# Scores and float32 folds as 64-row by 32-column products, and the first batch's k and v as two tensors

## The chip, the cores and the metric

The program runs on one core of a Trainium2 chip. The metric is the device time of one execution in microseconds (us); the kernel before takes 704.06 us, the median of three runs from 703.98 to 704.45. The core has a matrix engine (TensorE, PE in the profile; its weight loads are listed apart as PEld), two engines for elementwise work (VectorE is DVE, ScalarE is ACT), GpSimd (POOL) and SyncE (SP), whose queue issues most of the loads from memory. Each engine runs its own list of instructions in the order in which they stand there, and waits on semaphores for the others.

## The reference

Eight batches with eight heads of 576 tokens (head size 64) attend to 32 memory slots per head; the output goes through a feed-forward layer with g = h·cos(h).

```python
a = softmax(phi, axis=2)                       # phi: b, h, s, m (m = 32)
k_m = einsum('bhsm,bhsd->bhmd', a, k)          # memory keys
v_m = einsum('bhsm,bhsd->bhmd', a, v)          # memory values
scores = matmul(q, k_m.transpose(0, 1, 3, 2)) / sqrt(64)
attn_out = matmul(softmax(scores), v_m)        # b, h, s, d
x = attn_out as (b*s, 512)
h = x @ w_in                                   # 512 x 2048
out = (h * cos(h)) @ w_out                     # 2048 x 512
```

The two weights come as float64. phi, q, k and v are float32, and q, k and phi are scaled up so that both softmaxes are sharp.

## The kernel before, in words

The matrix of memory values is never applied to the attention weights. It is folded into `w_in` instead: for every batch the products v_m · w_in give a matrix of 256 rows (8 heads of 32 slots) by 2048 columns (`vw`, for the first group `vf`), and the softmaxed scores, transposed (`aT`), are multiplied by it directly. That is the first large product (`gemm1`, tile `hp`, L529 and L538). ACT and DVE then build h·cos(h) (`act`, `act_end`, tiles `u` and `gp`), and `gemm2` (tile `acc`, L577 and L582) multiplies by `w_out`. Group 0 does this in float32; the eleven later groups use pairs of float16 numbers, three products for one.

The 4608 tokens form 12 groups of 384. For each group the main loop takes 16 steps, one for each 128 of the 2048 hidden columns. A step issues `gemm1`, the two activations of `act`, and `gemm2` for the step four before it (`LAG`). Between the steps of group 0 the weights are converted from float64 to float32 (`to_float32`: a cast L147, an or L152, a square for the scale L155) in an order given by the list `todo`. Each converted piece of 256 columns of `w_in` is folded at once (`fold_first`, L500, tile `pvf`, copied to `vf` at L502). Batch 1 folds in float32 from the converted `w_in` (`fold` and `fold_psum`, L470); batches 2 to 7 fold with float16 pairs (L476).

The preparation of a batch is two generators, `memory` and `attend`, whose `yield`s cut them into 24 parts. Jobs with a first and a last step spread these parts over the steps of the groups before. `memory` makes the softmax of phi and the products with k and v (tile `psA`: 32 output rows per head, in four column quarters of the matrix array), divides by the sum (`den`, `X`), transposes (`tpx`), and writes the memory keys `km` and values `vm`. Both are laid out block-diagonally for pairs of heads: 128 rows by 64 columns per pair, where half of the entries are zeros that POOL sets beforehand (L300, L301). `attend` makes the scores (L381, tile `sc`): one product per pair of heads with all 128 rows of `km`, 64 output rows each, so that two products lie side by side in the array. It takes three blocks of tokens of 256, 256 and 64 (first batch: 256, 128 and 192), and the four products of one block lie in one bank of the pool `ps_s`. DVE transposes them back in 32 by 32 squares (L386), and the softmax over the 32 slots follows (L394 to L405).

The pool `ps_s` has two banks. `psA`, `tpx`, `sc`, `pvf` and `pv` all take their banks from it, and a new tile waits until the tile two before it has been read.

Before the loop stands the start-up, written out by hand: loads in the order phi, kv, q (first 384 tokens), `w_in` 0, `w_in` 1, the rest of q, `w_out` 0; then the first batch's `memory`, the conversion of `w_in` 0, the scores of its first 384 tokens, their softmax, `fold_first(0)` and `fold_first(1)`. Between them stand products of zeros (`warm`, L633) that keep the matrix engine busy. A scheduler then sets the final order on every engine by its own estimates; a few instructions are pinned.

## Time and profile before

The profiled execution took 702.34 us; the span of its core, from the first to the last instruction, is 700.6 us, so 1.7 us lie around it.

| what | value |
|---|---|
| median of the runs | 704.06 us |
| profiled execution | 702.34 us |
| span of the core | 700.6 us |
| PE busy | 685.8 us (98%) |
| DVE busy | 527.0 us (75%) |
| ACT busy | 500.0 us (71%) |
| POOL busy | 25.1 us (4%) |
| first product of the main loop (`hp`, group 0) starts | 31.03 us |
| granted clock over the span | 0.995 |

A busy share is the time in which at least one instruction of that engine ran. A float32 product appears as two records on PE, and products in different parts of the array overlap. The view by windows gives the busy time of each engine in stretches of the span; the chain of waits is followed back from the last instruction and gives start, length and what ran.

### The profile page before, as it was taken

The numbers are of one execution on the slowest core, as the hardware profiler recorded it, in microseconds if no ns is written. First come the engines' busy times: TensorE is split into PE (matmuls) and PEld (weight loads), VectorE is DVE, ScalarE is ACT, GpSimd is POOL, SyncE is SP. The second block draws the span as 40 slices with busy tenths as digits, with TensorE's granted clock in tenths as the row PEclk, the third lists the DMA queues.
The fourth block names the chain that finished last, engine by engine and source line by source line (L and its number), as shares of the span: only waits on it lengthen the run. The fifth ranks groups of instructions, "written<-read, shape, count | busy, mean of one in ns | idle before, by whom it ended". The sixth has DMA issues, their size and how long they took to land.

```text
span 700.6 us, 11828 instructions
## 1 busy us (share of the span) xinstructions
PE 685.8 (98%) x4597; PEld 364.0 (52%) x4597; DVE 527.0 (75%) x1125; ACT 500.0 (71%) x932; POOL 25.1 (4%) x42
## 2 busy tenths in 40 slices
PE   8799999999999999999999999999999999999997
PEld 3354445665454445665445455666445445665553
DVE  4788998998969866698658876599667976665652
ACT  1598998987876765877665965778666975765652
POOL 5020000000000000000001000000000000000000
PEclk9899999999999999999999999999999999999999
DMA  8996883336224100440105300160100100100101
GB/s 270 391 330 215 291 298 88 87 93 206 80 87 153 46 0 1 148 138 1 46 1 171 113 0 1 65 220 1 46 0 2 45 1 1 46 1 1 46 1 45
DMA packets 27863, 66.18 MB, mean 94 GB/s; under 512 B 2208, under 2 KB 12320, under 8 KB 25760
## 3 DMA queue, kind: packets, MB, share of 16 engines
q1 hardware_dynamic: 23344, 57.43, 24.7%
q10 hardware_dynamic: 4464, 8.00, 3.1%
q8 instruction: 36, 0.59, 0.3%
q14 instruction: 19, 0.16, 0.1%
HBM read 51.79 MB, written 9.44 MB: 87 GB/s over the span
## 4 chain that ended last, share of the span: by engine, by line
PE 68%; DVE 14%; ACT 13%; DMA 2%; issue 1%; SPq 0%; ACTq 0%; POOL 0%
PE acc L582 34%; PE hp L538 18%; PE acc L577 5%; ACT u L557 3%; PE hp L529 3%; DVE u L561 3%; DVE u L552 3%; PE psA L275 2%; DVE gp L564 2%; PE pv L476 2%; ACT gp L563 2%; PE sc L381 2%; DMA kv<-in_kv 1%; DVE vw L483 1%; ACT gp L549 1%
## 5 line engine op out<-in xcount | busy, mean ns | idle before, releaser
L582 PE MATMUL acc<-wo,gp 128*128 128x512 f16 x1584 | 371.4, 379 | 0.4 <-ACT ob L606 0.4
L582 PEld LDWEIGHTS <-gp 128*128 128x128 f16 x1584 | 153.4, 98 | 161.6 <-issue 2.8
L538 PE MATMUL hp<-aT,vw 128*128 128x192 f16 (+1 forms) x1440 | 202.8, 284 | 1.0 <-DVE u L561 0.9
L538 PEld LDWEIGHTS <-vw 128*128 128x128 f16 x1440 | 128.3, 98 | 77.8 <-issue 18.0
L557 ACT ACTIVATE u<-u,quarter 128x384 f32<-128x384 f32 x192 | 116.5, 613 | 65.7 <-DVE u L552 64.7
L561 DVE SCALAR_TENSOR_TENSOR u<-hp,u 128x384 f32<-128x384 f32 x176 | 96.6, 554 | 60.9 <-ACT u L557 60.3
L552 DVE SCALAR_TENSOR_TENSOR u<-hp,cu,gp 128x192 f32<-128x192 f32 (+1 forms) x240 | 118.9, 504 | 23.6 <-ACT gp L549 23.1
L549 ACT ACTIVATE gp<-hp,cu 128x192 int32<-128x192 f32 (+1 forms) x240 | 115.0, 490 | 27.3 <-PE hp L538 13.0
L564 DVE TENSOR_TENSOR gp<-u,gp 128x384 f16<-128x384 f32 x176 | 96.4, 553 | 42.9 <-ACT gp L563 41.9
L563 ACT CAST gp<-u 128x384 f16<-128x384 f32 x176 | 88.6, 509 | 54.0 <-DVE u L561 52.9
L577 PE MATMUL acc<-wo,gp 128*128 128x512 f32 x96 | 44.5, 598 | 0.0
L483 DVE SCALAR_TENSOR_TENSOR vw<-pv,vw 128x512 f16<-128x512 f32 x48 | 31.5, 685 | 3.0 <-ACT vw L482 2.9
L529 PE MATMUL hp<-aT,vf 128*128 128x384 f32 x64 | 25.3, 526 | 2.5 <-DVE aT L411 2.2
L482 ACT ACTIVATE vw<-pv 128x512 f16<-128x512 f32 x48 | 26.8, 588 | 1.1 <-PE pv L476 0.9
L577 PEld LDWEIGHTS acc<-wo,gp 128*128 128x128 f32 x96 | 17.5, 190 | 18.2 <-issue 16.0
L606 ACT ACTIVATE ob<-acc,os 128x512 f32<-128x512 f32 x27 | 17.8, 681 | 9.7 <-PE acc L582 7.1
L275 PE MATMUL psA<-kv,phi 128*32 128x129 f32 (+1 forms) x640 | 21.0, 275 | 1.2 <-DMA kv<-in_kv 0.5
L557 ACT ACT_TABLE_LOAD x17 | 21.8, 1283 | 0.3
L381 PE MATMUL sc<-q,km 128*64 128x256 f32 (+3 forms) x192 | 19.1, 334 | 1.2 <-DVE vw L483 0.7
L275 PEld LDWEIGHTS psA<-kv,phi 128*32 128x32 f32 (+1 forms) x640 | 16.4, 109 | 7.3 <-issue 2.1
L529 PEld LDWEIGHTS hp<-aT,vf 128*128 128x128 f32 x64 | 12.4, 203 | 14.2 <-issue 5.6
L381 PEld LDWEIGHTS sc<-q,km 128*64 128x64 f32 x192 | 11.7, 136 | 11.1 <-issue 3.2
(136 smaller groups left out, 524.6 us busy)
## 6 DMA issues: line engine op xcount, KB each, us to landing
kv<-in_kv SPq DMA_DIRECT2D x32, 516.0 KB, 6.9
raw_out<-in_w_out SPq DMA_DIRECT2D x8, 1024.0 KB, 5.8
q<-in_qT SPq DMA_DIRECT2D x7, 1152.0 KB, 5.5
out<-ob ACTq DMA_DIRECT2D x30, 256.0 KB, 2.1
raw_in<-in_w_in SPq DMA_DIRECT2D x6, 1024.0 KB, 10.3
phi<-in_phi SPq DMA_DIRECT2D x8, 512.0 KB, 5.9
w_in_sb<-w_in_parts SPq DMA_DIRECT2D x12, 256.0 KB, 4.1
kv<-in_kv SPq DMA_DIRECT2D x8, 258.0 KB, 7.8
```

What stands on the lines that cost most here:

```text
L275: nc.tensor.matmul(psA[32 * j:32 * (j + 1), g * KV:(g + 1) * KV], lhsT=a[:n, c, h * M:(h + 1) * M], rhs=kvs[c][:n, h * KV:(h + 1) * KV], s ...
L381: nc.tensor.matmul(sc[D * p:D * (p + 1), g * n:(g + 1) * n], lhsT=km[:, 2 * g + p], rhs=qt[:, 2 * g + p, t0:t0 + n], start=True, stop=True)
L529: nc.tensor.matmul(hp[:, :GT], lhsT=st["vf", q][:, g, fo * P:(fo + 1) * P], rhs=st["aTf"][:, g], start=(g == 0), stop=(g == 1))
L538: nc.tensor.matmul(hp[:, c0:c0 + n], lhsT=vw[:, wi, g, fo * P:(fo + 1) * P], rhs=aT[:, ai, g, c1:c1 + n], start=(k == 0), stop=(k == 5))
L549: ins = nc.scalar.activation(ni[:, c], hp[:, c], AF.Copy, scale=cu, bias=0.25)
L552: nc.vector.scalar_tensor_tensor(out=u[:, c], in0=hp[:, c], scalar=cu, in1=ni[:, c], op0=ALU.mult, op1=ALU.subtract)
L557: nc.scalar.activation(u, u, AF.Sin, scale=TWO_PI_BELOW, bias=quarter)
L561: nc.vector.scalar_tensor_tensor(out=u, in0=hp[:, :GT], scalar=2.0 ** -17, in1=u, op0=ALU.mult, op1=ALU.mult)
L563: nc.scalar.copy(gp[:, 0], u)
L564: nc.vector.tensor_tensor(out=gp[:, 1], in0=u, in1=gp[:, 0], op=ALU.subtract)
L577: nc.tensor.matmul(accs[grp][t], lhsT=gp[:, t * P:(t + 1) * P], rhs=wo[:, f + 1], start=(f == 0), stop=(f == NF - 1))
L582: nc.tensor.matmul(accs[grp][t], lhsT=gp[:, gi, t * P:(t + 1) * P], rhs=parts[:, wi], start=(f == 0 and gi == 0 and wi == 0), stop=(f == N ...
```

## The change

- **Products in eighths of the array.** `km` and `vm` lose their zeros: each head has 64 rows and 32 columns, even heads in one row half, odd heads in the other. A score product takes one head: 64 rows, 32 output rows. The two row halves write to different banks, so a block of scores takes both banks of `ps_s`. The blocks are two of 288 tokens (first batch: 384 and 192). The float32 folds (`fold_single`, for `fold_first` and for batch 1) are made in the same way, also with both banks; `fold_first` copies one bank on ACT and one on DVE. The number of these products doubles, each has half the rows and half the output rows. The float16 folds only take their heads in another order. The memsets of `km` and `vm` on POOL fall away.
- **k and v of the first batch.** Two new inputs hold k with its column of ones (65 columns per head) and v (64 per head). k is loaded before q and `w_in` 0, v behind `w_in` 0. `memory_first` makes the products with k alone, then `km`; the products with v follow behind the scores, in banks of the pool `ps_acc`, and `vm` is made on ACT. `den`, `X` and the scale of the values follow from the two parts.
- **Start-up.** The order by hand is written anew and has 43 products of zeros for 51; the conversion of `w_in` 0 is no longer pinned to the middle of `memory`.

The diff, cut to its core:

```diff
-BLK = [(0, 256), (256, 256), (512, 64)]
-BLK_FIRST = [(0, 256), (256, GT - 256), (GT, S - GT)]
+BLK = [(0, 288), (288, 288)]
+BLK_FIRST = [(0, GT), (GT, S - GT)]
...
+    def load_first(src, c0, c1):
+        if c0 == 0:
+            loads["kv", 0] = [ld.tile([P, H * KV], F32, tag="kv", name=f"kv_0_{c}", bufs=5) for c in range(5)]
+        for c, (s0, n) in enumerate(TCH):
+            nc.sync.dma_start(out=loads["kv", 0][c][:n, c0:c1], in_=src[s0:s0 + n])
...
+    def memory_first():
...
+        def products(ps, c, c0, w):
+            s0, n = TCH[c]
+            for g in range(2):
+                for j in range(4):
+                    h = 4 * g + j
+                    nc.tensor.matmul(ps[32 * j:32 * (j + 1), g * w:(g + 1) * w], lhsT=a[:n, c, h * M:(h + 1) * M],
+                                     rhs=kvs[c][:n, c0 + h * w:c0 + (h + 1) * w],
+                                     start=(c == 0 and g == 0), stop=(c == 4), skip_group_check=True)
+
+        psk = small_ps("psk")
+        for c in range(5):
+            products(psk, c, 0, K1)
+            yield
...
+        km = wk.tile([P, NP, M], F32, tag="km", name=f"km_{b}", bufs=1)
+        nc.scalar.mul(km[lo], tv[lo, :, 0], 1.0 / math.sqrt(D))
+        nc.vector.tensor_scalar(out=km[hi], in0=tv[hi, :, 1], scalar1=1.0 / math.sqrt(D), scalar2=None, op0=ALU.mult)
+        st["km", 0] = km
+        yield
+        psv = ps_acc.tile([P, DM], F32, tag="ps_acc", name="psv")
+        for c in range(5):
+            products(psv, c, H * K1, D)
+            if c == 2:
+                yield
+        X = wk.tile([P, 2, P], F32, tag="back", name="X_v", bufs=4)
+        for g in range(2):
+            nc.scalar.activation(X[:, g].rearrange("p (t d) -> p t d", t=2),
+                                 psv[:, g * D:(g + 1) * D].unsqueeze(1).broadcast_to([P, 2, D]), AF.Copy,
+                                 scale=den[:, g:g + 1])
...
     def memory(b):
...
-        km = wk.tile([P, NP, 2 * M], F32, tag="km", name=f"km_{b}", bufs=1)
-        vm = wk.tile([P, NP, 2 * M], F32, tag="vm", name=f"vm_{b}")
-        nc.gpsimd.memset(km, 0.0)
-        nc.gpsimd.memset(vm, 0.0)
+        km = wk.tile([P, NP, M], F32, tag="km", name=f"km_{b}", bufs=1)
+        vm = wk.tile([P, NP, M], F32, tag="vm", name=f"vm_{b}")
...
         def score_products(i):
             t0, n = BL[i]
-            sc_at[i] = sc = small_ps(f"sc_{b}_{t0}")
-            for g in range(2):
-                for p in range(2):
-                    nc.tensor.matmul(sc[D * p:D * (p + 1), g * n:(g + 1) * n], lhsT=km[:, 2 * g + p],
-                                     rhs=qt[:, 2 * g + p, t0:t0 + n], start=True, stop=True)
+            sc_at[i] = sc = [small_ps(f"sc_{b}_{t0}_{g}") for g in range(2)]
+            for c in range(NP):
+                for g in range(2):
+                    rows = slice(g * D, (g + 1) * D)
+                    nc.tensor.matmul(sc[g][M * c:M * (c + 1), :n], lhsT=km[rows, c],
+                                     rhs=qt[rows, c, t0:t0 + n], start=True, stop=True)
...
+    def fold_single(b, name, c0, n):
+        pv = [small_ps(f"{name}_{g}") for g in range(2)]
+        for c in range(NP):
+            for g in range(2):
+                rows = slice((1 - g) * D, (2 - g) * D)
+                nc.tensor.matmul(pv[g][M * c:M * (c + 1), :n], lhsT=st["vm", b][rows, c],
+                                 rhs=w_in_sb[rows, c, c0:c0 + n], start=True, stop=True)
         return pv
...
-        (nc.scalar.copy if j < 2 else nc.vector.tensor_copy)(out=st["vf", q][:, :, r * WS:(r + 1) * WS], in_=pv)
+        pv = fold_single(0, f"pvf_{j}", j * WS, WS)
+        nc.scalar.copy(out=st["vf", q][:, 0, r * WS:(r + 1) * WS], in_=pv[0][:, 0:WS])
+        nc.vector.tensor_copy(out=st["vf", q][:, 1, r * WS:(r + 1) * WS], in_=pv[1][:, 0:WS])
...
     load_phi(0)
-    load_kv(0)
+    load_first(k_first, 0, H * K1)
     load_q(0)
     load_w_in(0)
+    load_first(v_first, H * K1, H * KV)
     load_w_in(1)
...
-    convert_w_in(0, attention_rest)
-    for _ in mem:
-        pass
+    next(mem)
+    convert_w_in(0)
     first = attend(0)
     next(first)
-    warm(12)
+    warm(4)
+    next(mem)
+    warm(2)
+    next(mem)
+    next(mem)
+    warm(2)
     fold_first(0)
     warm(6)
     next(first)
+    for _ in mem:
+        pass
```

How the scheduler's order moves is shown at three places. The first is DVE around the first scores. `sc` are the scores, `at` their transposed copy, `raw_in` the raw `w_in` 0, `X_k` and `km` the scaled and transposed memory keys. Before, then with the change:

```order
L170 TENSOR_SCALAR ev_244<-ev_244 128x1
L386 STREAM_TRANSPOSE at_248<-sc_0_251 128x512
L147 CAST w_in_sb<-raw_in_117 128x4x256
L386 STREAM_TRANSPOSE at_248<-sc_256_257 128x256
L152 SCALAR_TENSOR_TENSOR w_in_sb<-raw_in_117,w_in_sb 128x4x256
L394 TENSOR_REDUCE rm_249<-at_248 128x24
L395 TENSOR_TENSOR at_248<-at_248,rm_249 128x768
```

```order
L284 TENSOR_SCALAR X_k<-psk,den_215 128x128 x2
L154 CAST w_in_sb<-raw_in_117 128x4x256
L295 TENSOR_SCALAR km_227<-tpx_k 64x128
L159 SCALAR_TENSOR_TENSOR w_in_sb<-raw_in_117,w_in_sb 128x4x256
L470 STREAM_TRANSPOSE at_234<-sc_0_0_237 128x384
L470 STREAM_TRANSPOSE at_234<-sc_0_1_238 128x384
L478 TENSOR_REDUCE rm_235<-at_234 128x24
L479 TENSOR_TENSOR at_234<-at_234,rm_235 128x768
```

The cast of `w_in` 0 now stands ahead of one half of `km`, so ahead of the scores, and the or behind it ahead of both transposes.

The second place is DVE in the second half of the same softmax (`rs` are its sums, `aT` the transposed weights for which the first `hp` waits). Before, then with the change:

```order
L399 TENSOR_REDUCE rs_250<-at_248 128x24
L152 SCALAR_TENSOR_TENSOR w_in_sb<-raw_in_119,w_in_sb 128x4x256
L400 TENSOR_SCALAR rs_250<-rs_250 128x24
L147 CAST wo<-raw_out_122 128x1024
L401 RECIPROCAL rs_250<-rs_250 128x24
L152 SCALAR_TENSOR_TENSOR wo<-raw_out_122,wo 128x1024
L405 TENSOR_TENSOR at_248<-at_248,rs_250 128x768
L411 STREAM_TRANSPOSE aT_247<-at_248 128x256 x2
```

```order
L485 RECIPROCAL rs_236<-rs_236 128x24
L579 COPY vf_317<-pvf_1_319 128x256
L489 TENSOR_TENSOR at_234<-at_234,rs_236 128x768
L159 SCALAR_TENSOR_TENSOR w_in_sb<-raw_in_124,w_in_sb 128x4x256
L495 STREAM_TRANSPOSE aT_233<-at_234 128x384 x2
L154 CAST wo<-raw_out_127 128x1024
L579 COPY vf_317<-pvf_1_349 128x256
L159 SCALAR_TENSOR_TENSOR wo<-raw_out_127,wo 128x1024
```

The conversion of `w_out` 0 (`raw_out`) has moved from ahead of `aT` to behind it; the or of `w_in` 1 still stands ahead of it.

The third place is PE at the start of group 0. Before, then with the change:

```order
L529 MATMUL hp_0_336<-aT_247,vf_275 128x384 x2
L529 MATMUL hp_1_375<-aT_247,vf_275 128x384
L500 MATMUL pvf_352<-w_in_sb,vm_226 64x256 x4
L381 MATMUL sc_384_358<-q_115,km_225 64x192 x4
L529 MATMUL hp_1_375<-aT_247,vf_275 128x384
L529 MATMUL hp_2_405<-aT_247,vf_275 128x384 x2
```

```order
L654 MATMUL acc_1_595<-wo,gp_0_392 128x512
L464 MATMUL sc_384_0_416<-q_115,km_227 32x192 x4
L654 MATMUL acc_2_596<-wo,gp_0_392 128x512
L464 MATMUL sc_384_1_417<-q_115,km_227 32x192 x4
L338 MATMUL top_450<-ident,nmx_448 128x128 x2
L606 MATMUL hp_4_585<-aT_233,vf_403 128x384
L556 MATMUL pvf_0_463<-w_in_sb,vm_302 32x256 x4
L606 MATMUL hp_4_585<-aT_233,vf_403 128x384
L556 MATMUL pvf_1_464<-w_in_sb,vm_302 32x256 x4
```

The score block of 192 tokens and one of the folds are cut in two by other work, each row half by itself; most other blocks stand with their two halves alternating product by product.

More of the change, by code (lines that the diff above doesn't have):

```diff
@@ L48, in attention_then_ffn @@
 @with_exitstack
-def attention_then_ffn(ctx: ExitStack, tc: tile.TileContext, phi, phiT, kv, qT, w_in, w_out, eye, out):
+def attention_then_ffn(ctx: ExitStack, tc: tile.TileContext, phi, phiT, kv, k_first, v_first, qT, w_in, w_out, eye, out):
     nc = tc.nc
@@ L420, in attend @@
         if b == 0:
-            for p in ((0, 1), (2,)):
-                for i in p:
-                    scores(i)
-                if p[0] == 0:
+            for i in range(2):
+                p = (i,)
+                scores(i)
+                if i == 0:
                     yield
@@ L429, in attend @@
                 normalize(p)
-                for i in p:
-                    back(i)
+                back(i)
                 yield
             return
-        score_products(0)
-        score_products(1)
-        score_back(0)
-        score_back(1)
+        scores(0)
         yield
-        score_products(2)
-        score_back(2)
+        scores(1)
         yield
@@ L443, in attend @@
             load_q(b + 1)
-        pieces = ((0,), (1, 2))
+        pieces = ((0,), (1,))
         for p in pieces:
@@ L466, in fold_psum @@
         pv = small_ps(f"pv_{b}_{q}_{g}")
[L467 to L477 removed]
+        for first in (True, False):
+            for c in range(NP):
+                nc.tensor.matmul(pv[M * c:M * (c + 1)], lhsT=(st["vp", b] if first else vl)[:, c, 1 - g],
+                                 rhs=st["w2", q][:, c, 1 - g], start=first, stop=not first, skip_group_check=True)
+        return pv
+    def fold_single(b, name, c0, n):
+        pv = [small_ps(f"{name}_{g}") for g in range(2)]
+        for c in range(NP):
+            for g in range(2):
+                rows = slice((1 - g) * D, (2 - g) * D)
+                nc.tensor.matmul(pv[g][M * c:M * (c + 1), :n], lhsT=st["vm", b][rows, c],
+                                 rhs=w_in_sb[rows, c, c0:c0 + n], start=True, stop=True)
         return pv
@@ L488, in fold @@
         st["vw", b, q] = vw
-        for g, pv in enumerate([fold_psum(b, q, g) for g in range(2)]):
-            split_fold(b, vw, g, pv)
+        pv = fold_single(b, f"pv_{b}_{q}", q * FS, FS) if b < 2 else [fold_psum(b, q, g) for g in range(2)]
+        for g in range(2):
+            split_fold(b, vw, g, pv[g])
     def fold_first(j):
@@ L761, in attention_then_ffn @@
         gemm2(*p)
-_INS = ["phi", "phiT", "kv", "qT", "w_in", "w_out", "eye"]
+_INS = ["phi", "phiT", "kv", "k_first", "v_first", "qT", "w_in", "w_out", "eye"]
 def kernel(**inputs):
@@ L781 @@
         "kv": kv.reshape(B, S, H * KV),
+        "k_first": np.concatenate([kt[0], np.ones((S, H, 1), k.dtype)], axis=2).reshape(S, H * K1),
+        "v_first": np.ascontiguousarray(vt[0]).reshape(S, H * D),
         "qT": np.ascontiguousarray(q.transpose(0, 1, 3, 2)).reshape(B, DM, S),
```

123 lines of the change are left out of this document (74 added, 49 removed).

## The prediction

> **What bounds the kernel now.** I read the page's first part, then the windows, then the chain of waits, and went into the timeline only where the chain leaves PE.
>
> ```profile
> PE 685.8 (98%) x4597; PEld 364.0 (52%) x4597; DVE 527.0 (75%) x1125; ACT 500.0 (71%) x932; POOL 25.1 (4%) x42
> ```
>
> ```profile
> 0.00:10.00 10.00, 8.73 (x28) 3.31 (x28) 6.47 (x17) 1.73 (x2) 8.91 (x13) 1.00 0.71 246
> 10.00:20.00 10.00, 8.81 (x115) 4.62 (x115) 3.82 (x15) 1.63 (x5) 0.35 (x1) 1.00 1.05 329
> 20.00:30.00 10.00, 6.18 (x33) 2.47 (x30) 8.75 (x12) 6.03 (x9) 0.00 (x0) 0.88 1.02 405
> 30.00:40.00 10.00, 8.97 (x35) 5.09 (x36) 6.95 (x13) 7.32 (x12) 2.05 (x2) 0.77 1.07 337
> 40.00:60.00 20.00, 20.00 (x146) 10.73 (x144) 16.56 (x37) 17.00 (x29) 2.16 (x2) 1.00 0.76 276
> 60.00:100.00 40.00, 39.52 (x132) 18.08 (x131) 38.22 (x83) 38.34 (x60) 1.32 (x4) 1.00 0.85 304
> 100.00:140.00 40.00, 40.00 (x237) 21.99 (x237) 36.98 (x74) 36.28 (x73) 0.31 (x1) 1.00 0.36 91
> 140.00:200.00 60.00, 59.52 (x421) 33.35 (x419) 53.59 (x117) 49.32 (x92) 0.97 (x3) 1.00 0.36 111
> 200.00:700.00 500.00, 494.07 (x3462) 264.34 (x3460) 355.71 (x764) 342.36 (x658) 9.06 (x16) 1.00 0.15 50
> ```
>
> The columns behind the length are busy PE, weight loads, DVE, ACT, POOL, then the granted clock, the DMA share and GB/s. Three stages show. Up to 31 us PE waits for the first batch. From there to 140 us PE is full, but DVE and ACT are nearly full too (from 60 to 100 us 38.2 and 38.3 of 40). From 200 us on PE is full and the other two have 30% to spare. So PE time removed late is time gained. Removed between 40 and 140 us it is gained only as far as ACT and DVE can follow.
>
> ```profile
> 3.80 9.91 DMA kv<-in_kv
> 17.97 1.52 PE sc L381 x16
> 22.18 1.04 PE pvf L500 x8
> 31.03 3.90 PE hp L529 x6
> 35.95 0.65 PE sc L381 x8
> 45.46 2.47 PE psA L275 x80
> 57.60 1.88 PE sc L381 x16
> 60.53 0.38 PE sc L381 x8
> 83.77 1.08 PE pvf L500 x8
> 87.62 1.87 PE pv L470 x8
> ```
>
> These are pieces of the chain, start and length. At the start it hangs on the load of k and v, later on PE alone.
>
> **The products in eighths.** Eight records of 256 columns cost 1.04 and 1.08 us, eight of 512 columns 1.87, sixteen of 256 columns 1.88. All fit one line: 0.25 us for each run of such products, and 0.81 us for eight records of 256 columns with two tiles side by side. With four tiles the 80 `psA` records of 129 columns would cost 0.25 + 0.81·(129/256)·10·(2/4) = 2.29 us and took 2.47, so four tiles run side by side almost wholly. No row here shows tiles in two row halves at once. The bounds: eight at once (a quarter of the two-tile time per record), or four at once with the halves one behind the other. I take eight, because `psA` lost so little from two to four, and because each half has a bank of its own.
>
> - Scores of a batch: two blocks of 16 records of 288 columns, each 0.25 + 0.81·2·(288/256)/4 = 0.71 us, 1.41 in all, for 1.88 + 0.38 = 2.26 us: −0.85 us. At the other bound 2·(0.25 + 0.91) = 2.32: +0.06.
> - Folds of batch 1, four: 0.25 + 0.81·2·2/4 = 1.06 for 1.87: −0.81 each, −3.2. Other bound: 0.
> - `fold_first` in the loop, six: five at 0.25 + 0.81·2/4 = 0.66 for 1.06, −2.0. The sixth is cut by `hp` into two runs of one half, each 0.66: +0.25.
> - The first batch's 192 tokens, also cut in two: 2·(0.25 + 0.81·0.75·2/4) = 1.11 for 0.65: +0.46.
> - Batches 2 to 7: 6·0.85 = 5.1, less two blocks which the new order cuts in two, each 2·0.71 for 0.71, so 1.4, and two more runs of column-tiled products between full ones (0.2): −3.5.
>
> Sum up to 140 us: −3.2 − 2.0 − 0.85 + 0.25 + 0.46 = −5.3 us; behind it −3.5. If the halves do not overlap, only the cuts and runs stay: about +1.2 us.
>
> The Trainium skill (TensorE: Matmul & The Clock Gate, Part 3, measured speedup) gives 3.07 for four row tiles, which I read as an estimate of 1.75 for each doubling of rows instead of 2. By it the sum would be some 1 us smaller; no run here shows it yet.
>
> **The start.**
>
> ```profile
> 9.56 1.53 ACT L265 ACTIVATE phi<-phi 128x512 f32<-128x512 f32 x3 [2.77 <-DVE phi L259]
> 10.24 0.65 PE L275 MATMUL psA<-kv,phi 128*32 128x129 f32 x16
> 14.94 0.64 PE L275 MATMUL psA<-kv,phi 64*32 64x129 f32 x16
> 19.73 0.70 DVE L147 CAST w_in_sb<-raw_in 128x1024 f16<-128x1024 bf16 x1
> 20.69 1.18 DVE L152 SCALAR_TENSOR_TENSOR w_in_sb<-raw_in,w_in_sb 128x1024 uint32<-128x1024 uint32 x1
> 21.79 0.94 DVE L394 TENSOR_REDUCE rm<-at 128x24 f32<-128x768 f32 x1
> 22.77 0.96 DVE L395 TENSOR_TENSOR at<-at,rm 128x768 f32<-128x768 f32 x1
> 23.76 0.84 ACT L427 ACTIVATE at<-at 128x768 f32<-128x768 f32 x1
> 24.63 0.95 DVE L399 TENSOR_REDUCE rs<-at 128x24 f32<-128x768 f32 x1 [0.91 <-ACT at L427]
> 25.86 1.23 DVE L152 SCALAR_TENSOR_TENSOR w_in_sb<-raw_in,w_in_sb 128x1024 uint32<-128x1024 uint32 x1 [0.27 <-ACT w_in_sb L147]
> 27.08 0.77 DVE L147 CAST wo<-raw_out 128x1024 f16<-128x1024 bf16 x1
> 27.94 1.17 DVE L152 SCALAR_TENSOR_TENSOR wo<-raw_out,wo 128x1024 uint32<-128x1024 uint32 x1
> 29.02 0.95 DVE L405 TENSOR_TENSOR at<-at,rs 128x768 f32<-128x768 f32 x1
> 30.01 1.16 DVE L411 STREAM_TRANSPOSE aT<-at 128x256 f32<-128x256 f32 x4
> ```
>
> The identity, phi and k are 1.85 MB, and 2.46 MB are through by 10 us, so k is there before the exponential of phi (9.56 to 11.09). The products with k start at 10.24 as before, wait for no load, and end at some 12.4 us for 15.6. Then `den`, `X`, transpose and `km` took 2.4 us. New on that way: DVE casts `w_in` 0 ahead of `km`. Up to `w_in` 0 it is 3.69 MB, at 329 GB/s behind 10 us landed at 13.7, as late as 14.6 if the same lag applies as before (17.3 by this count, and it was cast at 19.73); cast 0.70, half of `km` 0.3. PE also has four products of v's first part ahead of the scores, another 0.26 MB. Scores at about 15.4 us for 17.97.
>
> Behind them on DVE: the or of 1.18, both transposes (1.16 like `aT`'s), maximum 0.94, subtraction 0.96, to about 20.2 us. ACT scales the products with v ahead of the exponential. v is complete after 4.87 MB, 17.3 to 18.2 us, its last products and the scaling end by 19.8, so they just fit. Exponential 0.84, sum 0.95, small work 0.5, a copy of `vf` 0.4, product 0.95, or of `w_in` 1 1.23, `aT` 1.16: first `hp` at 26 us for 31.03. **Gain 5 us** (bounds 3 and 6.5: `w_in` 0 or v a microsecond later; the clock, which fell to 0.77 behind the idle PE of 20 to 30 us, staying up). Of it 1.9 us are the conversion of `w_out` 0, only moved behind `aT`: late next are the first `u` and `gp`. PE has four `hp` in the new order to cover that.
>
> The next load that can bind is batch 1's k and v: loads are full from 10 to 50 us with the same bytes, and `psA` of batch 1, now at 45.46, would move to some 40.5, where 13.0 MB must be in: by the windows 13.2 MB at 40 us. It just fits, at worst 1 us.
>
> **What ACT and DVE let through.** Potential to 140 us: 5 + 5.3 = 10.3 us. ACT is busy 6.03 + 7.32 + 17.00 + 38.34 + 36.28 = 105.0 us between 20 and 140.
>
> ```profile
> L557 ACT ACT_TABLE_LOAD x17 | 21.8, 1283 | 0.3
> L502 ACT COPY vf<-pvf 128x512 f32<-128x512 f32 x2 | 1.2, 585 | 0.8 <-PE pvf L500 0.8
> L502 DVE COPY vf<-pvf 128x512 f32<-128x512 f32 x6 | 4.1, 686 | 1.0 <-PE pvf L500 0.9
> ```
>
> New on ACT: eight copies of 256 columns (by proportion and some fixed part 0.4) for two of 0.585, +2.0; two more table loads in the new order, +2.6; scaling the products with v, +0.7. That is 110 us, in a stretch that starts some 5 us earlier, at 15: 125 us without any idle time. With an idle time of 8 us (it was 15) the mark of 140 us comes at 133. I take 7 of the 10.3 us.
>
> Sum: 7 + 3.5 = 10.5 us on the profiled execution of 702.34 us, so 691.8. The median lies 1.7 us above that execution, so **693.5 us**.
>
> **Rivals.**
> - *Everything is gained* (ACT and DVE follow): 10.3 + 3.5 = 13.8, and 1.7 more if the clock stays up: 689. For it: ACT and DVE idle a third of 20 to 40 us. Against: from 60 to 100 us they have 4% left, and ACT gets work.
> - *ACT becomes the bound*: its stretch keeps 12 us of its idle time, so the mark moves 3 us, and 3.5 follow: 697.5. The Trainium skill (TensorEngine Tiling (Array Packing), PSUM Bottleneck) warns of this: tiling does not speed up emptying the banks. Full ACT windows agree.
> - *The halves do not overlap*: +1.2 on the products, 4 of the start: 701.
> - *Slower, both banks at once*: `ps_s` has two banks, and each fold and score block now needs both, so PE, in order, waits for the copies on ACT and DVE. A conversion ahead of the copy is 1.2 us. Fifteen such runs to 140 us at 1 us each are 15 us: 704.06 − 10.5 + 15 = 708.5. It decides above 0.7 us per run. Against: the folds come a step of 4 us apart and the order was planned with those banks.
>
> **How the numbers follow.** Chances: forecast 0.58, everything gained 0.12, ACT bound 0.12, no overlap 0.10, both banks 0.08. A change under 0.2% (1.4 us) could not be told from none. Faster: 0.58 + 0.12 + 0.12 and 0.06 of the no-overlap case, 0.88; the other 0.04 of it the same; slower 0.08. The forecast's own range is 690 to 697; with everything gained below and the ACT case and part of the no-overlap case above it is 687.5 to 699.5.
>
> **What would show it.** In the profile after: scores of 16 records in about 0.7 us on PE, folds of batch 1 in 1.06 (1.2 and 1.9 would mean halves one behind the other); first `hp` near 26 us; the cast of `w_in` 0 ended by 15.3 us; PE below full from 60 to 100 us with ACT above 39 of 40; from 200 us on PE full as now. Idle PE ahead of `pvf` and `sc`, released by the copies, would be the case of both banks. A first `hp` after 29 us, or psA of batch 1 waiting for its load by more than 2 us, would make the prediction wrong.

## The result

The change is faster by less than half of what was forecast: 699.0 us (median of four runs, 696.75 to 699.32) against 704.02 us of the kernel before on the same chip, a ratio of 0.9933 with a 95% interval from 0.9919 to 0.9946. That is a gain of 5.0 us where the sum said 10.5. The profiled execution is the fastest of the four, 696.75 us with a span of 694.9 us, 5.6 us under that of before.

The first part of the page after the change, busy time by engine:

```profile
PE 676.0 (97%) x4829; PEld 351.5 (51%) x4829; DVE 526.0 (76%) x1118; ACT 501.5 (72%) x936; POOL 20.5 (3%) x26
```

PE has 9.8 us less to do than before (685.8), but the span is shorter by 5.7 us only. The view by windows of the changed kernel, in the columns of the prediction (length, busy PE, weight loads, DVE, ACT, POOL, clock, DMA share, GB/s), shows where PE is no longer full:

```profile
10.00:20.00 10.00, 8.81 (x192) 4.35 (x192) 6.42 (x12) 2.79 (x7) 0.00 (x0) 1.00 1.04 375
20.00:30.00 10.00, 8.01 (x54) 3.54 (x54) 7.94 (x17) 6.95 (x13) 0.35 (x1) 1.00 1.03 406
30.00:40.00 10.00, 8.20 (x57) 3.34 (x58) 8.00 (x12) 8.01 (x15) 3.61 (x2) 1.00 1.06 340
60.00:100.00 40.00, 39.29 (x196) 17.22 (x196) 37.08 (x81) 38.53 (x64) 0.70 (x2) 1.00 0.87 288
100.00:140.00 40.00, 38.94 (x270) 22.56 (x268) 39.31 (x79) 38.16 (x79) 0.00 (x0) 1.00 0.41 103
140.00:200.00 60.00, 58.26 (x490) 31.65 (x488) 52.59 (x113) 49.18 (x90) 0.35 (x1) 1.00 0.34 105
200.00:694.00 494.00, 485.99 (x3391) 255.97 (x3388) 350.49 (x750) 338.07 (x645) 6.95 (x9) 1.00 0.15 50
```

Two things differ from the rows of before. The clock stays at 1.00 between 20 and 40 us in this execution, where it was 0.88 and 0.77; in a second one it fell there too, as the part on the prediction shows. And behind 100 us PE has idle time, 8.0 us in the last row where it had 5.9, the end behind the last product included in both.

The start and the products came out as the sum had them. From the timeline of the changed kernel, start and length first:

```profile
14.42 0.75 DVE L154 CAST w_in_sb<-raw_in 128x1024 f16<-128x1024 bf16 x1 [0.16 <-DMA raw_in<-in_w_in]
15.37 1.05 PE L464 MATMUL sc<-q,km 64*32 64x384 f32 x16
25.41 1.56 PE L606 MATMUL hp<-aT,vf 128*128 128x384 f32 x4
55.15 0.72 PE L464 MATMUL sc<-q,km 64*32 64x288 f32 x16
64.94 0.66 PE L556 MATMUL pvf<-w_in_sb,vm 64*32 64x256 f32 x16
98.49 1.09 PE L556 MATMUL pv<-w_in_sb,vm 64*32 64x512 f32 x16
```

The scores of the first batch start at 15.37 us (forecast 15.4), the first `hp` at 25.41 (forecast 26, before 31.03). A score block takes 0.72 us (0.71 forecast), `fold_first` 0.66 (0.66), a fold of batch 1 1.09 (1.06). So with the fixed 0.25 us of a run set apart, all eight tiles run at once, the two row halves too. The first two runs came dearer, and why stays open: the score block of 384 columns took 1.05 us where the same line gives 0.86, and the `fold_first` ahead of the loop 0.94. The Trainium skill (TensorE: Matmul & The Clock Gate, Part 3, measured speedup) gives 3.07 for four row tiles. The prediction read this, as an estimate, as 1.75 for a doubling on top of the fixed part, and the score block would then have taken 0.25 + 1.82/3.5 = 0.77 us, which the trace does not show. Taken over a whole run, fixed part included, a fold became 1.87/1.09 = 1.72 times as fast, so the measurement does not speak against that figure.

The gain was then lost again. Group 2 starts (its first `acc`) at 175.7 us before and at 168.8 after, a gain of 6.9 us, and the last `acc` ends at 696.3 and 691.1, a gain of 5.2. The windows between these marks, before and then after:

```profile
175.70:696.30 520.60, 518.27 (x3587) 276.72 (x3585) 375.52 (x804) 361.76 (x692) 9.37 (x17) 1.00 0.14 49
```

```profile
168.80:691.10 522.30, 517.01 (x3627) 272.09 (x3625) 375.20 (x798) 363.00 (x687) 6.95 (x9) 1.00 0.14 49
```

Behind group 2's start the changed kernel is slower by 1.7 us. The forecast had 3.5 us of gain for batches 2 to 7; the scores of batch 2 stand ahead of this mark, so some 2.7 us were to come behind it. PE's busy time there falls by 1.3 us only, and its idle time rises from 2.3 to 5.3 us.

The groups of PE's records from group 1 on show that the products themselves did become shorter (busy time, mean of one record, idle time before them); of before:

```profile
L381 PE MATMUL sc<-q,km 128*64 128x256 f32 (+1 forms) x144 | 14.4, 335 | 0.9 <-DVE vw L483 0.7 <-issue 0.2
L470 PE MATMUL pv<-w_in_sb,vm 128*64 128x512 f32 x16 | 3.9, 605 | 0.0
```

and of the change:

```profile
L464 PE MATMUL sc<-q,km 64*32 64x288 f32 x192 | 11.3, 415 | 1.6 <-DVE vw L563 1.6
L556 PE MATMUL pv<-w_in_sb,vm 64*32 64x512 f32 x32 | 2.2, 601 | 0.0
```

That is 3.1 us less for the scores of batches 2 to 7 and 1.7 us less for two folds of batch 1. The 11.3 us hold some waiting that counts as busy. Seven of the twelve late score blocks (batches 2 to 7) take 0.72 us and two, cut in two by other work, twice 0.69, but three take 0.99, 1.31 and 1.25 us (at 208.8, 379.6 and 539.0 us), 1.4 us too much together. In each of them PE stops within the block; for the one at 379.6 the lines under "What the waits are" show that one bank was free and the other not yet. What PE waited for from 110 us to the end (total, times, longest), before:

```profile
PE hp L538 <- DVE u L561: 0.9, 2, 0.7
PE sc L381 <- DVE vw L483: 0.7, 1, 0.7
PE psA L275 <- ACT phi L265: 0.4, 1, 0.4
PE acc L582 <- ACT ob L606: 0.4, 1, 0.4
PE sc L381 <- issue: 0.2, 1, 0.2
```

and after the change:

```profile
PE sc L464 <- DVE vw L563: 1.6, 1, 1.6
PE acc L659 <- ACT ob L683: 1.5, 2, 0.8
PE psA L362 <- ACT phi L353: 1.4, 1, 1.4
PE hp L615 <- DVE u L638: 1.4, 3, 0.5
PE acc L659 <- ACT ob L671: 0.9, 2, 0.7
PE pv L547 <- DVE at L470: 0.5, 1, 0.5
```

2.6 us of waits became 7.3. The experiments ask why. For each I give the sum of this view ("late waits") beside the time.

### The profile page after: what moved, and what is told of

Its sections match the earlier page's. It is cut to its first block, busy times and chain, and to the rows that moved or that the text cites. A ratio compares the mean times of both kernels' runs of the same rounds, so it can differ in the third digit from the quotient of the medians.

```text
span 694.9 us, 12245 instructions
## 1 busy us (share of the span) xinstructions
PE 676.0 (97%) x4829; PEld 351.5 (51%) x4829; DVE 526.0 (76%) x1118; ACT 501.5 (72%) x936; POOL 20.5 (3%) x26
## 4 chain that ended last, share of the span: by engine, by line
PE 60%; DVE 18%; ACT 17%; DMA 2%; issue 2%; SPq 1%; POOL 0%; ACTq 0%; POOLq 0%
PE acc L659 36%; PE hp L615 18%; PE pv L547 3%; ACT u L634 3%; DVE u L629 2%; DVE u L638 2%; DVE gp L641 2%; ACT gp L626 2%; ACT L634 1%; ACT gp L640 1%; DVE vw L563 1%; DMA kv<-in_v_first 1%; ACT raw_out L162 1%; PE psA L362 1%; ACT vw L562 1%
## 5 line engine op out<-in xcount | busy, mean ns | idle before, releaser
L683 ACT ACTIVATE ob<-acc,os 128x512 f32<-128x512 f32 x27 | 17.8, 681 | 8.9 <-PE acc L659 7.1
L362 PE MATMUL psA<-kv,phi 128*32 128x129 f32 (+1 forms) x560 | 17.8, 275 | 1.5 <-ACT phi L353 1.4
L362 PEld LDWEIGHTS psA<-kv,phi 128*32 128x32 f32 (+1 forms) x560 | 14.5, 109 | 5.9 <-ACT phi L353 3.2
L464 PE MATMUL sc<-q,km 64*32 64x288 f32 (+2 forms) x256 | 15.2, 415 | 2.0 <-DVE vw L563 1.6
L470 DVE STREAM_TRANSPOSE at<-sc 128x288 f32<-128x288 f32 (+2 forms) x32 | 14.1, 463 | 1.5 <-PE sc L464 1.5
```

Source lines behind the costliest of these rows:

```text
L362: nc.tensor.matmul(psA[32 * j:32 * (j + 1), g * KV:(g + 1) * KV], lhsT=a[:n, c, h * M:(h + 1) * M], rhs=kvs[c][:n, h * KV:(h + 1) * KV], s ...
```

## The experiments

The theories, by the letters that the expectations use. **A**: a late score block takes both banks of `ps_s`, and so loses in waits what it saves in products. **B**: the late products are worth what the sum says, and the loss has another place. **C** and **F**: in the stretches where a batch is prepared VectorE (C) or ScalarE with its table loads (F) is full. **G**: VectorE stands in line for the loads of phi. **H**: VectorE is full in group 1. **D**: the waits come from the order in which the instructions stand in the queues, whatever the engines' load. The runs called light or without late tables leave out or replace a part of the work, so that a load on one engine falls.

| run | time, us | before on that chip | ratio, 95% | late waits, us |
|---|---|---|---|---|
| change, first and second time | 699.0; 698.65 | 704.02; 704.49 | 0.9933 (0.9919–0.9946); 0.992 (0.9906–0.9935) | 7.3; 7.3 |
| e1 old late scores | 699.78 | 703.28 | 0.9933 (0.9916–0.9949) | 7.1 |
| e2 old start | 703.73 | 703.28 | 1.0006 (0.9994–1.0018) | 8.9 |
| e3 folds two steps later | 699.87 | 703.28 | 0.9939 (0.9924–0.9955) | 9.1 |
| e4 second block one part later | 702.9 | 703.28 | 1.0002 (0.9981–1.0023) | 10.3 |
| e6 before, light VectorE | 701.12 | 704.49 | 0.9956 (0.994–0.9971) | 1.1 |
| e7 change, light VectorE | 696.93 | 704.49 | 0.9899 (0.9882–0.9915) | 7.4 |
| e8 e1, light VectorE | 697.42 | 704.49 | 0.9903 (0.9885–0.9921) | 4.5 |
| e9 before, no late tables | 706.82 | 703.9 | 1.0045 (1.0027–1.0063) | 4.9 |
| e10 change, no late tables | 701.73 | 703.9 | 0.9969 (0.9957–0.9981) | 9.8 |
| e11 e1, no late tables | 700.1 | 703.9 | 0.9948 (0.9932–0.9965) | 8.4 |
| e12 maximum later | 698.26 | 703.4 | 0.9925 (0.9908–0.9942) | 7.5 |
| e13 low part of w_out on GpSimd | 721.2 | 703.4 | 1.0251 (1.0233–1.027) | 23.4 |
| e14 the same in before | 721.08 | 703.4 | 1.0255 (1.0235–1.0275) | 17.5 |
| e15 e12 and e13 | 719.02 | 703.4 | 1.0227 (1.0199–1.0256) | 24.6 |
| e16 group 1 light | 702.13 | 703.15 | 0.9972 (0.9957–0.9987) | 11.0 |
| e17 before, group 1 light | 704.35 | 703.15 | 1.0018 (1.0008–1.0029) | 4.1 |
| e18 e1, maximum later | 698.49 | 703.15 | 0.9933 (0.9919–0.9947) | 6.1 |

The granted clock enters these times beside the waits. In some executions it falls behind a wait of PE: in the profiled ones of e10 (at 115 and 385 us), of e16 (at 155 and 385 us) and of e12 (at 380 us) it stands at 0.66 to 0.75 over five microseconds, right behind waits of 1.4 to 2.3 us, and each such fall is some 1.7 us of clock lost (what is missing to 1.00, times its length). The profiled executions of the change have a like wait at 380 us (1.64 and 1.5 us) and kept 1.00 there. The ten executions of e16 divide by it: four with a clock of 0.999 or 1.000 over the span took 699.7 to 700.2 us, six with 0.995 took 702.0 to 703.9. All six of e10 had 0.993 to 0.995, and in e13 to e15 it was 0.980 to 0.990.

### Start or products: e1 and e2

e1 is the change, with scores and order of heads as before for batches 2 to 7:

```diff
+BLK_LATE = [(0, 256), (256, 256), (512, 64)]
+            if b >= 2:
+                sc_at[i] = sc = small_ps(f"sc_{b}_{t0}")
+                for g in range(2):
+                    for p in range(2):
+                        nc.tensor.matmul(sc[D * p:D * (p + 1), g * n:(g + 1) * n], lhsT=km[:, 2 * g + p],
+                                         rhs=qt[:, 2 * g + p, t0:t0 + n], start=True, stop=True)
```

> The changed kernel with the scores of batches 2 to 7 as before (128x64 products, three blocks, one bank each, and the float16 folds in the head order that fits). Theory A (behind 110 us the change wins about 3 us of score time and loses as much to PE waits for both banks of ps_s and to cut blocks): taking the new late scores away changes little, within 1.2 us of the changed kernel, and the PE gaps ahead of sc behind 110 us fall from some 3 us to under 1.5. Theory B (the score gain is real and the lost time comes from elsewhere, from ACT and DVE work that the earlier start pushes on): 2.5 to 3.5 us slower than the changed kernel.

e2 is the other half: all the products of the change, with the loads and the start-up of before (`memory` for batch 0 too, no `k_first` and `v_first`):

```diff
-def attention_then_ffn(..., phi, phiT, kv, k_first, v_first, qT, ...)
+def attention_then_ffn(..., phi, phiT, kv, qT, ...)
-    mem = memory_first()
+    mem = memory(0)
```

> The changed kernel's products with the start of before (one kv tensor, memory as before, the old order by hand). If the start and the products add up (start 5.6 us by the traces, group 0 1.5, behind it a loss of 1): 703 to 704, no faster than before by more than 1 us. If group 0 is held by ACT, so that an earlier start spoils what the products save there (PE busy in group 0 fell by 4 us, its length by 1.5): 700.5 to 702, and group 0 shorter than before by 3 us or more.

e2 is no faster than before: its products brought 1.3 us up to group 2's start (174.4 against 175.7 us), but its last `acc` ends 1.7 us later (698.0 against 696.3), so 2.9 us were lost between. A part of that zero can be clock: in its profiled execution 5.1 us of clock were lost between 25 and 40 us, in that of before 3.4. e1 stands 0.8 us above the change's first time and 1.1 above its second, within what A had expected (1.2), though PE still waits 2.3 us ahead of its score blocks, where A had under 1.5. By difference, then, nearly the whole gain comes with the new start, and the late score products are worth about 1 us, if anything, of the 3.1 that they became shorter. The start alone, with all the old products, was not run.

e1 shows one way in which time is lost late. From 186 us of before on its instructions on PE, DVE, ACT and SyncE stand in the same order as in before, so the two traces can be laid over each other: e1 is 5.06 us ahead at 196 us and 2.68 us from 466 us to the end. The loss falls in three jumps, 0.90, 0.81 and 0.60 us, each where DVE takes the maximum over the next batch's phi (L225, in e1 L233). The first, from the timelines of before and of e1:

```profile
212.47 0.69 DVE L225 TENSOR_TENSOR mx<-phi 128x512 f32<-128x512 f32 x1 [0.34 <-DMA phi<-in_phi]
```

```profile
208.31 0.69 DVE L233 TENSOR_TENSOR mx<-phi 128x512 f32<-128x512 f32 x1 [1.24 <-DMA phi<-in_phi]
```

DVE waits in line for a load that nobody else needs for some microseconds, and everything behind it comes later. Here the order cannot be the cause, since it is that of before. The load takes longer in e1, a median of 6.5 us from issue to landing for 6.0 in before. In the change it takes 5.4 us, and DVE waits there once, 1.0 us at 372 us.

### Other distances: e3 and e4

```diff
-            folds.setdefault(use - before + 4 * q + 1, []).append((b, q))
+            folds.setdefault(use - before + 4 * q + 3, []).append((b, q))
```

> The changed kernel with every fold of batches 1 to 7 issued two steps later, so that the folds' banks and the second score block of the next batch no longer meet where they do now (PE waited 1.64 us there for batch 5). Theory A: 1 to 2.5 us faster than the changed kernel, with the gap ahead of the second score block of batch 5 gone. Theory B: within 0.7 us of it.

e4 moves one empty part of `attend` from the end to between the two score blocks:

```diff
         scores(0)
         yield
+        yield
         scores(1)
...
-        yield
         back(1)
```

> The changed kernel with the second score block one part later in the job (an empty part moved from the end of the softmax to between the two blocks), so that its two banks have longer to come free. Theory A: 0.5 to 2 us faster than the changed kernel, fewer score blocks of over 0.9 us on PE. Theory B: within 0.7 us.

A had both faster than the change. e3 stands 0.9 us above it, and e4 loses nearly all its gain; its two executions at a clock of 1.000 took 701.3 and 701.4 us. In both the waits moved to other places and grew.

### Is VectorE full? e5 to e8

The score products lie where DVE is busiest, so I took work off it there, for batches 2 to 7, with the change itself run again beside it:

```diff
         def shift(blocks):
+            if b >= 2:
+                return
```

> The change itself, beside the three runs below on the same chip: 698.5 to 699.5 us, about 4.5 us under before, as on the first chip. If it stands at 699.8, as the version with the old late scores did, the two are equal and the late score products are worth nothing.

> The kernel before, with the shift of the softmax (maximum reduce and subtract, about 3 us of VectorE per batch) left out for batches 2 to 7; exp is taken of the unshifted scores. This takes some 18 us off VectorE, all of it in the stretches in which a batch is prepared, and nothing off TensorE. Theory C (VectorE is full in those stretches, and sets them once TensorE has less to do): before waits only 2.75 us on TensorE after group 0, so it can gain at most that, 701 to 702.5 us. Rival D (the waits come from the order of the instructions, not from VectorE being full): no change, 703.3 us.

> The change with the same shift left out for batches 2 to 7. Theory C: the 7.9 us that TensorE waits after group 0 fall to 2 or 3, and the time falls by 4 to 6 us to 693 to 695 us, so that the difference between the two light kernels is 8 us or more, where it is 5 with the shift. Rival D: the waits stay, 698 to 699 us, and the difference stays at 5 us or less.

> The change with the scores and float16 folds of batches 2 to 7 as before, and the same shift left out. With the shift this version equalled the change (699.8 us). Theory C: without VectorE in the way the late products are worth their 3.2 us on TensorE, so this stands 2.5 to 3.5 us above the light change, 696 to 697.5 us. Rival D: equal to the light change within 1 us.

C's numbers do not come for the change: e7 lies between C's and D's. The light change keeps its late waits (7.4 us), the distance to the light kernel before shrinks from 5.8 to 4.2 us instead of growing to 8, and the old late scores are again worth as much as the new ones (697.42 and 696.93). For the kernel before they do come: e6 gained 3.4 us and its late waits fell from 2.6 to 1.1, where D had no change. The test of C is not a clean one either, for the edit had a side effect: with other durations the scheduler put the exponentials of the two score halves apart, and table loads rose from 36 to 44, some 10 us more on ACT (one group of the change and the same one of e7):

```profile
L634 ACT ACT_TABLE_LOAD x18 | 23.1, 1283 | 0.3
```

```profile
L636 ACT ACT_TABLE_LOAD x22 | 28.2, 1283 | 0.4
```

### Are the table loads in the way? e9 to e11

Several waits stand behind a table load on ACT. With a copy in place of the exponential for batches 2 to 7, these runs load no table late; what they compute is no softmax:

```diff
-            nc.scalar.activation(a[:n, c0:c1], a[:n, c0:c1], AF.Exp)
+            nc.scalar.activation(a[:n, c0:c1], a[:n, c0:c1], AF.Exp if b < 2 else AF.Copy)
...
-            nc.scalar.activation(piece(p)[0], piece(p)[0], AF.Exp)
+            nc.scalar.activation(piece(p)[0], piece(p)[0], AF.Exp if b < 2 else AF.Copy)
```

> The kernel before, with the exponentials of batches 2 to 7 (of phi and of the scores) replaced by a copy on ScalarE: the same instructions in shape and number, but no change of the activation table behind batch 1, so 24 loads of 1.28 us less on ScalarE; what is computed is no softmax. Theory F (the waits of TensorE behind group 0 stand behind table loads on ScalarE): before waits 2.75 us there, so it can gain about that, 700.5 to 702 us. Rival D (the waits are of the instructions' order whatever ScalarE has to do): no change.

> The change, with the same replacement. Theory F: of the 7.9 us that TensorE waits behind group 0 at most 2 are left, and the late products give what the sum had for them, so 692 to 694 us, at least 8 us under the same version of before. Rival D: 4 us or more of the waits stay, 696 to 698.5 us, and the distance stays at 5 us.

> The change with the old late scores and float16 folds, with the same replacement. Theory F: 2.5 to 3.5 us above the change with that replacement, 695.5 to 697 us, since the late score products then count. Rival D: within 1 us of it, as with the tables and as without the shift.

ACT lost 35 us of work (466.9 us busy for 501.5), and none of the three became faster. The kernel before is slower by 0.45%, and e11 equals e1. The change is slower by some 3 us than its other runs; the two falls of the clock in its profiled execution are 3.4 us, so this is the clock more than the work. Theory F falls, for it had 692 to 694 us for e10, though D's 696 to 698.5 was missed too. The three largest waits of e10:

```profile
PE sc L464 <- DVE vw L563: 3.7, 3, 2.0
PE acc L659 <- ACT ob L671: 2.2, 2, 1.9
PE pv L547 <- DVE at L470: 1.2, 2, 0.7
```

PE now stands three times ahead of a score block, for 3.7 us, where it was once and 1.6 us in the change.

### The loads of phi, and group 1: e12 to e18

```diff
-            if i == e - 6 and NT <= b + 1 < B:
+            if i == e - 3 and NT <= b + 1 < B:
```

> The change, with the maximum over phi of batches 4 to 7 given out three steps later. VectorE takes its work in line, and in the change it stands 1.0 us at 372 us for the load of phi; three steps are about 10 us, so no maximum waits for a load. Theory G (these stalls are what TensorE's waits behind 200 us come from): 1.5 to 3 us faster than the change, 696 to 697 us, with the 1.64 us wait of the scores of batch 5 gone. Rival D (the waits only move with the order): the same as the change within 1 us.

e12 stands 0.4 us under the change's second time, inside both intervals, and the wait ahead of the scores of batch 5 is still 1.59 us. So theory G does not hold for the change. It does for e1, where the three jumps are most of what it loses late.

Of group 1, where the change fills DVE (9.65, 9.92, 9.94 and 9.91 of 10 us from 110 to 150 us; before 8.30, 8.76, 9.96, 9.85), no run so far took anything away. e13 (the change) and e14 (before) give a part of it to GpSimd, and e15 adds e12's edit:

```diff
-        nc.vector.scalar_tensor_tensor(out=parts[:, 1], in0=wo[:, f + 1], scalar=s, in1=parts[:, 0],
-                                       op0=ALU.mult, op1=ALU.subtract)
+        nc.gpsimd.tensor_scalar(out=wo[:, f + 1], in0=wo[:, f + 1], scalar1=s, scalar2=None, op0=ALU.mult)
+        nc.gpsimd.tensor_tensor(out=parts[:, 1], in0=wo[:, f + 1], in1=parts[:, 0], op=ALU.subtract)
```

> The change, with the low float16 part of w_out (16 pieces in group 1, 0.73 us of VectorE each, 11.7 us) made on GpSimd by a multiply and a subtract in place of one VectorE instruction. Theory H (VectorE is full from 60 to 160 us in the change, so the shorter folds of batch 1 could not be collected in group 1): VectorE falls below 9 of 10 us in group 1, the waits of 0.95 us at its start and 1.45 us at the phi products of batch 2 go, and the time falls by 2 to 3 us to 695.5 to 697 us. Rival D: no change within 1 us.

> The kernel before with the same piece on GpSimd. Theory H: its TensorE waits only 0.4 us in group 1, so at most 0.5 us faster, 703 to 704 us, and the distance to the run above grows from 5 to 7 us or more. Rival D: unchanged, the distance stays at 5 us.

> The change with both edits, meant to beat both kernels: 694 to 696 us if G and H hold, 698 to 699 us under rival D.

All three are slower than before by 15.6 to 17.8 us, a part of it at a lower clock. In e13 GpSimd takes 2.9 us for what took DVE 0.74, and one group of DVE's own instructions became longer beside it: `gp<-u,gp`, 0.55 us in the change, has a mean of 0.84 us here, while `u<-hp,u` kept its 0.55. Groups of e13, POOL and then DVE in group 1:

```profile
L203 POOL TENSOR_SCALAR wo<-wo,s_out 128x512 f32<-128x512 f32 x16 | 26.1, 1631 | 24.6 <-ACT wo L202 17.7 <-ACT gp L626 6.9
L204 POOL TENSOR_TENSOR wo<-wo 128x512 f16<-128x512 f32 x16 | 20.1, 1254 | 1.3
```

```profile
L641 DVE TENSOR_TENSOR gp<-u,gp 128x384 f16<-128x384 f32 x18 | 15.1, 843 | 7.5 <-ACT gp L640 7.5
```

That tells nothing of H, so the same work was made shorter on DVE itself, in the change (e16) and in before (e17), by a copy of the high parts in place of the low ones:

```diff
-        nc.vector.scalar_tensor_tensor(out=parts[:, 1], in0=wo[:, f + 1], scalar=s, in1=parts[:, 0],
-                                       op0=ALU.mult, op1=ALU.subtract)
+        nc.vector.tensor_copy(out=parts[:, 1], in_=parts[:, 0])
...
-        nc.vector.scalar_tensor_tensor(out=parts[:, 1, c], in0=src, scalar=s, in1=parts[:, 0, c],
-                                       op0=ALU.mult, op1=ALU.subtract)
+        nc.vector.tensor_copy(out=parts[:, 1, c], in_=parts[:, 0, c])
```

> The change, with the low float16 parts of w_in and w_out, made in group 1, replaced by copies of the high parts on VectorE: the same instructions in number, order of inputs and outputs, but a float16 copy in place of a float32 multiply and subtract, 32 of them at 0.74 us (23.7 us of VectorE in group 1) made shorter; the products then use wrong low parts. Theory H (VectorE is full from 60 to 160 us in the change, and so the shorter folds of batch 1 are lost in group 1): the waits at the start of group 1 and at the phi products of batch 2 (2.4 us together) go for the most part, 695.5 to 697 us. Rival D: within 1 us of the change.

> The kernel before with the same replacement. Theory H: TensorE waits only 0.4 us there, so at most 0.5 us faster, and the distance between the two grows from 5 to about 7 us. Rival D: unchanged, distance 5 us.

H falls too. In e16 DVE is down to 6.52 and 7.08 of 10 us at the start and the end of that stretch (windows of e16, with the fall of the clock in the third):

```profile
110.00:120.00 10.00, 8.41 (x62) 4.24 (x61) 6.52 (x17) 9.55 (x21) 0.00 (x0) 1.00 0.34 105
140.00:150.00 10.00, 10.00 (x72) 6.45 (x71) 7.08 (x17) 7.79 (x19) 0.00 (x0) 1.00 0.49 107
150.00:160.00 10.00, 7.73 (x99) 4.63 (x98) 7.16 (x15) 7.75 (x14) 0.00 (x0) 0.83 0.38 112
```

and yet PE waits longer than in the change for the exponential of batch 2, 2.27 us for 1.45, and 1.5 us at the start of the group. The kernel is some 3 us slower than the change with less to do, of which two thirds are clock: its four executions at 0.999 or 1.000 took 699.7 to 700.2 us. The last run is e1 with e12's edit:

> The change with the old late scores and float16 folds, and the maximum over phi given out three steps later, so that the phi loads no longer hold VectorE (3.3 us of stalls there, against 1.0 in the change). Theory A (a late score block that takes both banks of the small pool loses by waiting what it saves in products): 1 to 2 us under the change, 696.5 to 697.7 us, and so the fastest version. Rival (the late products are worth their 3.2 us, and the stalls cost nothing): 699 to 700 us as without the edit.

698.49 us lies between the two expectations, 1.3 us under e1, with DVE still waiting 2.4 us for loads of phi. It does not decide between A and its rival. No run that does all the work beats the change by what can be measured: e12 stands at 0.9925 (0.9908–0.9942). The light e7 and e8, at 0.990, leave the shift of the softmax out.

### What the waits are

With a lighter DVE, a lighter ACT or a lighter group 1 the late waits of kernels with the new start or the new products stay between 4.5 and 11.0 us, and those of the kernel before between 1.1 and 4.9. So less load does not remove them, though it can lessen them (e6 and e8). At single places the traces can be read. The scores of batch 5 wait for banks in which the folds of batch 4 lie. In the change (start and length):

```profile
376.04 0.39 PE L547 MATMUL pv<-w_in_sb,vl 128*32 128x512 f16 x4
376.37 1.15 PE L615 MATMUL hp<-aT,vw 128*128 128x384 f16 x6
377.35 0.59 PE L659 MATMUL acc<-wo,gp 128*128 128x512 f16 x2
378.22 1.08 ACT L562 ACTIVATE vw<-pv 128x512 f16<-128x512 f32 x2
378.84 1.29 DVE L563 SCALAR_TENSOR_TENSOR vw<-pv,vw 128x512 f16<-128x512 f32 x2
379.59 1.31 PE L464 MATMUL sc<-q,km 64*32 64x288 f32 x16 [1.64 <-DVE vw L563]
380.18 0.18 PEld L464 LDWEIGHTS sc<-q,km 64*32 64x32 f32 x14 [0.46 <-DVE vw L563]
```

and in before:

```profile
383.59 0.39 PE L476 MATMUL pv<-w_in_sb,vl 128*32 128x512 f16 x4
383.91 1.15 PE L538 MATMUL hp<-aT,vw 128*128 128x384 f16 x6
384.89 1.89 PE L582 MATMUL acc<-wo,gp 128*128 128x512 f16 x8
385.95 1.07 ACT L482 ACTIVATE vw<-pv 128x512 f16<-128x512 f32 x2
386.74 1.28 DVE L483 SCALAR_TENSOR_TENSOR vw<-pv,vw 128x512 f16<-128x512 f32 x2
387.48 0.45 PE L381 MATMUL sc<-q,km 128*64 128x64 f32 x8 [0.70 <-DVE vw L483]
```

The scores here are the second of two blocks in the change and the third of three in before. From the fold over the copies to the scores the way is about as long in both, 3.2 us from 376.4 and 3.5 us from 384.0. But PE's list holds two products of `acc` in between where it held eight, 1.3 us less, and PE waits 0.94 us more. The last line of the change adds what the two banks cost on top: the first of DVE's two copies lets the block begin, and the weights for 14 of its 16 records come only behind the second, so the block takes 1.31 us for 0.72. The same at batch 2: DVE's subtraction starts 1.8 us after the end of `top` in the change (149.05), 0.6 us in before (154.89). So at these places the wait is a way through the queues of two or three engines, and its length is set by what stands ahead in them. This fits D, but D's own numbers were missed too: e6 was faster and e9 slower where it had no change, and e10 and e16 were slower than it had. The reading was made at these places, not shown by a run in which the order alone was changed; whether one cause lies behind all the waits stays open.

## Why the prediction was wrong

**The products: right.** 0.25 us for a run and a quarter of the two-tile time gave 0.71, 0.66 and 1.06 us; measured 0.72, 0.66 and 1.09. The bound at which the halves come one behind the other is out. Two readings on the way were off without moving the result. The 0.65 us for before's block of 192 tokens is the piece of it on the chain; the whole run took 0.82, so the cut of that block cost some 0.2 us less than the sum has. And the estimate of 1.75 for a doubling, worked through the same list, makes the sum some 1.5 us smaller, not some 1.

**The start: right.** Scores at 15.37 for 15.4, the cast of `w_in` 0 ended at 15.17 for 15.3, first `hp` at 25.41 for 26; the gain is 5.6 us, inside the bounds of 3 and 6.5, and 5.1 us in the second profiled execution of the change (25.9). The upper bound's reason held as well in the first execution, where the clock stayed up. The 14.6 us for `w_in` 0 at the latest does not follow from the figures beside it, whose lag would be 2.4 us and would give 16.1; the cast waited for the load until 14.42, so that term was right by luck. `psA` of batch 1 came at 43.66 us, not 40.5, and waited for no load.

**What ACT and DVE let through: near in one execution, with help of the clock.** 7 of 10.3 us was the term, without the 1.7 us that the prediction gives for a clock that stays up. At group 2's start, a mark that has the scores of batch 2 in it as well, the gain is 6.9 us in the first execution, where the clock stayed up. In the second, with that mark at 171.2 us, it is 4.4 against the same profile of before. There the clock fell between 30 and 40 us (windows of e5):

```profile
30.00:35.00 5.00, 3.06 (x7) 1.46 (x6) 2.96 (x4) 4.99 (x7) 0.00 (x0) 0.77 1.06 369
35.00:40.00 5.00, 5.00 (x41) 1.55 (x40) 3.68 (x7) 3.31 (x8) 3.55 (x2) 0.88 1.08 304
```

Its first `hp` came 0.5 us later than in the first execution and its `psA` of batch 1 1.7 us later (45.40 for 43.66), so 1.2 of the 2.5 us between the two marks were lost in that stretch. So the 6.9 beside the 7 is in part luck. ACT did not pass 39 of 40 us from 60 to 100 us (38.53); DVE was the fuller one from 100 to 140 us (39.31). The late next was as named, the first `u` and `gp`, which PE waited for 1.9 us.

**The late term: wrong, and the step is this one:** "From 200 us on PE is full and the other two have 30% to spare. So PE time removed late is time gained." The late score products became 3.1 us shorter on PE, where 3.5 had been worked out, and none of it shows in the time. From group 2's start to the end the change lost 1.7 us on before (1.5 in the second execution), where some 2.7 had been added: 4.4 of the 4.9 us by which the profiled execution misses its 691.8. In place of the gain stand waits of PE, 7.3 us from 110 us on for 2.6, and 1.4 us of waiting within three blocks. The 30% is a mean over 500 us. It says that the other engines can do the work, not that each piece comes in time for a PE that arrives a microsecond earlier. e1 and e2 say the same: with the old late scores the change is about 1 us slower, and all the shorter products with the old start are worth 1.0006. What sets the waits one by one is read at some places only and otherwise stays open.

**The rivals.** The ACT case gives 697.5 us, nearest to the result, but by luck: it moves the early mark by 3 us, which moved by 6.9 and 4.4, and counts the 3.5 us of late products as gained, which were lost. Both banks at once cost little up to 140 us, 0.3 us ahead of one score block and 0.4 within another, where the prediction had 1 us at each of fifteen runs. Behind it they cost something that the late term put at nothing: the 1.4 us within the three blocks, and a share of the one wait of 1.64 us ahead of `sc` where before had 0.70.

## What to carry to other kernels

A full PE beside engines with idle time on average does not make PE time worth its length: look at the waits one by one, at how many microseconds of PE's own list lie between a product and the product that needs its evicted result, and take off what the edit removes there. Where a scheduler sets the order from its estimates, any change of durations gives a new order, and its waits are a cost to count even if every product becomes shorter. A wait can cost more than its length, because the granted clock can fall behind it; so times are to be compared at the same clock before a slower run is put down to its edit. A single wait can stand behind an instruction that nobody needs yet, like a maximum that waits for a load in the middle of a full queue.

## What the runs showed of the hardware

- Products of 64 rows by 32 columns in both row halves and four column quarters, each half with a bank of its own, run eight at a time once a fixed 0.25 us a run is set apart: 16 records of 288 columns in 0.72 us, where two tiles side by side would take 2.07, an estimate from before's runs.
- The granted clock fell behind waits of PE of 1.4 to 2.3 us in e10, e12 and e16, to 0.66 over five microseconds (1.7 us of clock lost), and not behind one of 1.64 us in the change. In e16 executions of 699.7 to 700.2 us had a clock of 0.999 or 1.000 over the span, those of 702.0 to 703.9 one of 0.995.
- A tiled block that writes to two banks began when the first was free and stopped within itself for the second: 1.31 us for 0.72, counted as busy.
- GpSimd took 1.63 us to scale 128x512 float32 values and 1.25 us to subtract them into float16, and beside it DVE's `gp<-u,gp` took half as long again (0.84 for 0.55 us), `u<-hp,u` no longer than without (0.56 for 0.55).
- A float16 copy of 128x512 took DVE 0.295 us, where the float32 multiply and subtract takes 0.74.
- The same load of phi took 5.4 us in the change and 6.5 us in e1, from issue to landing; why was not tried.
